# Local-attention value windows: 42 rows per block instead of 38, and one load for both heads' edge blocks

## The chip, the cores and the metric

The kernel runs on one core of a Trainium2 chip, as one program. The metric is device time in microseconds (us), the median of several executions. Five engines work beside each other, each through its own instruction list in a fixed order: PE (matrix products), DVE (vector work), ACT (activation functions, copies), POOL (some vector sums) and SP, which only issues DMA transfers here. A core has 16 DMA engines.

## The reference

Three stages follow one another, and each feeds the next.

```python
# attention: q, k, v are (2 batches, 8 heads, 576 positions, 64), float32; factor 4
out_d     = softmax(scale * q_d @ k_d.T) @ v_d      # q_d, k_d, v_d: means over 4 positions
scores    = where(|i - j| < 4, scale * q @ k.T, -1e9)
out_local = softmax(scores) @ v
x = repeat(out_d, 4) + out_local                    # 1152 tokens x 512
# first feed-forward
h = x @ w_in                                        # 512 -> 2048
y = (h * tanh(softplus(h))) @ w_out                 # 2048 -> 512
# second feed-forward
out = (silu(y @ w_gate) * (y @ w_val)) @ w_out2     # 512 -> 1536 -> 512
```

The weights arrive in 64-bit floats; x, q, k and v in 32-bit ones.

## The kernel before

**Attention.** The heads are taken in pairs: 2 batches x 4 pairs. For a pair, `prep` (L403) loads q and k (`qk`, L429, 1024 runs of 256 bytes over 128 partitions), the last 64 positions of all heads (`qr`, L400, 64 partitions x 8 heads) and the values for the coarse attention (`vq`, L434, 72 partitions x 4 runs of 1 KB). PE transposes q and k (L463), ACT copies them out (L480), DVE and POOL form the sums over four positions (L491, L447), and `down` (L512) does the coarse attention.

**Local attention.** A position sees only its neighbours within three places, so the positions are cut into 18 blocks of 32 (`BLK`), and a block needs 38 keys and values (`WIN`): its 32 and three at either side. `ks_of(t)` is where the window of block t begins; block 0 has nothing to its left and block 17 nothing to its right, so their windows are shifted. Six blocks form a unit, three units (u = 0, 1, 2) a head pair. `duo` (L636) works on two units at once: scores (L667), softmax on DVE and ACT, transposes (L699), the products with the values (`o_local`, L712), and the sum with the coarse part (L725), which is written to the token tile `xy`.

**The value windows.** `load_windows` (L605) is called for each batch and each half of its pairs (four calls in all). A call makes six loads, 24 in all: a load fetches the windows of one unit for both heads of a pair, one window row per partition, so that a block's 38 rows lie in 38 partitions (0 to 37 or 64 to 101), and the six blocks lie side by side. Row and block are 256 bytes (64 floats) each. For one head, one DMA takes all blocks whose windows are regular ("inner": five for u = 0 and u = 2, six for u = 1), and a further DMA takes the shifted edge block. That makes four DMAs for u = 0 and u = 2, two for u = 1: 80 in all, all issued by SP on L618. The tile is `vw` where the two units share a pair and `vj` where they don't; each has two buffers.

**The weights.** `convert` (L267) loads 512 KB of a weight matrix into `raw` (L282 or L287, on SP), of which there are three buffers; ACT and DVE turn the 64-bit numbers into a pair of reduced-precision tiles (L299 to L335). The products of the first feed-forward (L771 to L773) begin while attention still runs.

**Order.** `Plan.run` is a list scheduler that runs when the kernel is built. It knows a cost for each step, a due time (`want`) and the free buffers, and writes one fixed order for each engine. A load's cost on SP comes from this function, so a load of windows counts `us_dma(12 * WIN, 256)`, 0.73 us:

```python
def us_dma(runs, size):
    return max(0.475, runs * max(size, 512) / 320e3)
```

On SP the windows stand between `prep`'s loads and the first `raw` loads, in that fixed order. Where PE would be idle in the plan, short products of zeros (`warm`, L1106) are put in; they are instructions like others, 179 in all.

Of the kernel before, what the change touches and what calls it, by code (L numbers as in the profile page):

```python
# [20 lines left out]
BLK = 32  # L21
WIN = BLK + 6
EXN = 3
NTOK = 1152
PC = 384
PIECES = [(i * PC, PC) for i in range(3)]
# [56 lines left out]
class Plan:  # L83
# [9 lines left out]
    def add(self, eng, fn, deps=(), want=0.0, new=(), use=(), table=None):  # L93

        o = Op(eng, fn, deps, want, list(new), list(new) + list(use), table)
        self.ops.append(o)
        return o
# [72 lines left out]
def attention_moe_kernel(  # L170
# [12 lines left out]
    nc = tc.nc  # L183
    PE, ACT, DVE, POOL = nc.tensor, nc.scalar, nc.vector, nc.gpsimd
    B, H, S, D = q.shape
# [19 lines left out]
    plan = Plan()  # L205
    E_PE, E_POOL, E_SP = "PE", "POOL", "SP"
# [8 lines left out]
    def us_act(n, psum=False):  # L215
        return n / 1200 + (0.051 if psum else 0.093)

    def us_dma(runs, size):
        return max(0.475, runs * max(size, 512) / 320e3)
# [12 lines left out]
    def ring(pool, tag, n):  # L232
        if tag not in rings:
            rings[tag] = Ring(n)
        return rings[tag]

    def buf(pool, shape, dt, tag, n):

        b = Buf(ring(pool, tag, n))

        def make():
            tiles = b.ring.tiles
            if b.slot not in tiles:
                tiles[b.slot] = (late[pool] if isinstance(pool, str) else pool).tile(
                    shape, dt, tag=f"{tag}{b.slot}", name=f"{tag}{b.slot}", bufs=1)
            b.tile = tiles[b.slot]
            return b.tile

        b.make = make
        return b  # L250
# [6 lines left out]
    
    x_buf = buf(xp, [128, 2, 4, NTOK], F32R, "xy", 1)
    x_buf.ring.give(x_buf)
# [89 lines left out]
    masks = acst.tile([128, 9, WIN], BF16, name="masks")  # L349
    exs = acst.tile([128, EXN, 6, 64], F32, name="exs")  # L350

# [38 lines left out]
    def ks_of(t):  # L390
        return min(max(BLK * t - 3, 0), S - WIN)
# [213 lines left out]
    def load_windows(b, y, w):  # L605

        def load(vw, p, u, r0, h0, first):
            ts = [6 * u + j for j in range(6)]
            inner = [j for j in range(6) if ks_of(ts[j]) == BLK * ts[j] - 3]

            def f(e):
                if first:
                    vw.make()
                for h in range(2):
                    s_ = v[b, 2 * p + h]
                    row = vw.tile[r0:r0 + WIN, h0 + h]
                    for j0, n in [(inner[0], len(inner))] + [(j, 1) for j in range(6) if j not in inner]:
                        nc.sync.dma_start(out=row[:, j0:j0 + n, :],  # L618
                                          in_=bass.AP(tensor=s_.tensor, offset=s_.offset + ks_of(ts[j0]) * D,
                                                      ap=[[D, WIN], [BLK * D, n], [1, D]]))  # L620
            return f

        for u0, u1, apart in (((0, 1, False), (2, 2, True)), ((0, 0, True), (1, 2, False)))[b]:
            vw = buf(ld, [128, 2 if apart else 4, 6, 64], F32, "vj" if apart else "vw", 2)
            o = None
            for p in range(2):
                for k, u in enumerate((u0, u1)):
                    if not apart or p == k:
                        h0 = 0 if apart else 2 * p
                        o = plan.add({E_SP: us_dma(12 * WIN, 256)}, load(vw, 2 * y + p, u, 64 * k, h0, o is None), [o], w,  # L630
                                     [] if o else [vw], [vw] if o else [])
                        wins[b, 2 * y + p, u] = (vw, o, h0)

    ex_ring = ring(None, "ex", EXN)

# [131 lines left out]
    att_ops = []  # L767
    GSHAPE = [128, 2, NTOK]

# [25 lines left out]
    def l1(f, i, want):  # L795
        n = PC
        if f not in HB:
            HB[f] = buf(thp, [128, NTOK], F32, "H", RING)
            HB[f].ops, HB[f].first = [], None
# [17 lines left out]
    def mish(f, h, want):  # L817

        add = plan.add
        g = G[f] = buf("g", GSHAPE, F32R, "G", 7)  # L820
        t = buf("g", [128, NTOK], F32, "T", 2)

# [18 lines left out]

        o = add({"ACT": us_act(NTOK)}, tanh, h.ops + tanhs[-1:] + att_ops, want + 1.79, [t], [h], "exp")
        tanhs.append(o)
# [4 lines left out]
        for f, h, g, t, want, atan, sin, mult, hi, lo in batch:  # L848
            o = add({"ACT": us_act(NTOK) + 0.09}, atan, [o, o_small], want + 10.41, use=[t], table="trig")
            o = add({"ACT": us_act(NTOK) + 0.09}, sin, [o], want + 10.41, use=[t], table="trig")  # L850
# [145 lines left out]
    w = 10.0  # L996
    prep(0, 0, w)
    load_windows(0, 0, w)
    duo([(0, 0, 0), (0, 1, 0)], (w, w + 2.0), True)
    w += 2 * 2.0  # L1000
# [4 lines left out]
    duo([(0, 2, 0), (0, 2, 1)], (w, w + 2.0), True)  # L1005
    w += 2 * 2.0
    load_windows(0, 1, w)
    duo([(0, 0, 2), (0, 1, 2)], (w, w + 2.0), True)
    w += 2 * 2.0
# [3 lines left out]
    t_p0 = w  # L1013
    prep(1, 0, w + 2.0)
    load_windows(1, 0, w)
    duo([(0, 2, 2), (0, 2, 3)], (w, w + 2.0), False)
    w += 2 * 2.0
# [125 lines left out]
```

## Time and profile before

| | us |
|---|---|
| median of 3 executions | 562.24 (561.42 to 565.15) |
| the profiled execution | 563.22 |
| its span, first to last instruction | 561.4 |
| PE busy in the span | 521.1 (93%) |
| DVE busy | 380.9 (68%) |
| ACT busy | 274.3 (49%) |
| POOL busy | 23.3 (4%) |

The profiled execution is 1.0 us above the median; 1.8 us of it lie outside the span. An engine's busy share is a mean over stages: the profile's strip of 40 slices shows PE near full from about 126 us to the end, while attention, ahead of that, has slices with PE, DVE and ACT all half idle. SP has no busy time of its own in the profile: the time of its DMA-issuing instructions stands in the chain of waits and in the timeline as "SPq". The rows that the prediction uses stand below, behind the diff.

### The profile page before, as it was taken

The page shows a single profiled execution, that of the slowest core. Times are in us where ns is not written, and L with a number is a line of the kernel's source. Part 1 is how long each engine was busy: PE and PEld are TensorE (multiplying, and loading weights), DVE is VectorE, ACT ScalarE, POOL GpSimd, SP SyncE. Part 2 cuts the span into 40 slices and gives each one's busy share as a digit, 9 for nine tenths or more (in the row PEclk, how much of TensorE's full clock was granted, in tenths as well). Part 3 has the DMA queues.
Part 4 walks back from the last instruction along what each step waited for, and adds up shares of the span by engine and source line. Part 5 has one row for each costly group of instructions (what it writes and reads, how often), then busy time and mean ns, then how long its engine had stood idle before and what let it go on. Part 6 is the DMA issues. An engine that isn't in the chain of part 4 may idle for free.

```text
span 561.4 us, 9942 instructions
## 1 busy us (share of the span) xinstructions
PE 521.1 (93%) x3991; PEld 486.4 (87%) x3991; DVE 380.9 (68%) x764; ACT 274.3 (49%) x567; POOL 23.3 (4%) x41
## 2 busy tenths in 40 slices
PE   9949694749998999999999999999999999999997
PEld 7737474638998999999999999999999889998885
DVE  4817563536998999898886999866666249733321
ACT  3925453405699985973892454333343244321000
POOL 3303110200000000000000000000000000000000
PEclk9966869567999999999999999999999999999999
DMA  9355261441432125321512133433222204100022
GB/s 181 81 98 106 67 152 40 119 126 52 151 114 75 39 85 177 114 75 39 188 41 73 37 114 113 132 102 103 77 76 76 75 1 149 39 0 1 0 76 93
DMA packets 58749, 48.52 MB, mean 86 GB/s; under 512 B 31184, under 2 KB 53968, under 8 KB 58704
## 3 DMA queue, kind: packets, MB, share of 16 engines
q1 hardware_dynamic: 58704, 47.90, 29.9%
q8 instruction: 31, 0.51, 0.4%
q14 instruction: 14, 0.11, 0.1%
HBM read 45.53 MB, written 2.36 MB: 85 GB/s over the span
## 4 chain that ended last, share of the span: by engine, by line
PE 70%; SPq 17%; DMA 4%; ACT 4%; issue 2%; DVE 1%; POOL 1%; ACTq 0%; POOLq 0%
PE b L771 19%; PE b L773 18%; PE b L772 18%; SPq L618 14%; PE b L966 4%; PE b L967 4%; PE b L965 4%; DMA vq<-in_v_dram 2%; SPq L429 1%; PE b L712 1%; POOL vd L447 1%; DMA raw<-in_moe_w_out_dram 1%; DMA raw<-in_moe_w_in_dram 1%; SPq L282 1%; ACT T L830 1%
## 5 line engine op out<-in xcount | busy, mean ns | idle before, releaser
L771 PE MATMUL b<-xy,wt 128*128 128x384 f32 x480 | 163.6, 341 | 0.0
L773 PE MATMUL b<-xy,wt 128*128 128x384 f32 x480 | 162.5, 339 | 0.0
L772 PE MATMUL b<-xy,wt 128*128 128x384 f32 x480 | 162.5, 338 | 0.0
L771 PEld LDWEIGHTS b<-xy,wt 128*128 128x128 f32 x480 | 91.8, 191 | 0.5 <-issue 0.2
L772 PEld LDWEIGHTS b<-xy,wt 128*128 128x128 f32 x480 | 91.8, 191 | 0.0
L773 PEld LDWEIGHTS b<-xy,wt 128*128 128x128 f32 x480 | 91.7, 191 | 0.0
L772 PE MATMUL b<-G,wt 128*128 128x384 f32 x192 | 64.2, 335 | 1.8 <-DVE G L840 1.8
L773 PE MATMUL b<-G,wt 128*128 128x384 f32 x192 | 64.1, 334 | 0.0
L771 PE MATMUL b<-G,wt 128*128 128x384 f32 x192 | 64.1, 334 | 0.0
L299 ACT ACTIVATE cw<-raw 128x512 f32<-128x512 f32 x61 | 40.6, 669 | 36.0 <-DVE wt L335 16.6
L226 ACT ACTIVATE G<-H 128x384 fp32r<-128x384 f32 (+1 forms) x40 | 24.0, 605 | 64.0 <-DVE H L937 43.2
L335 DVE TENSOR_TENSOR wt<-cw,wt 128x512 fp32r<-128x512 f32 x68 | 46.3, 690 | 2.6 <-ACT wt L226 1.4
L314 DVE SCALAR_TENSOR_TENSOR cw<-raw,cw 128x512 uint32<-128x512 uint32 x68 | 46.7, 693 | 0.5
L319 DVE SCALAR_TENSOR_TENSOR cw<-raw,cw 128x512 uint32<-128x512 uint32 x68 | 46.5, 691 | 0.3
L967 PE MATMUL b<-wt,G 128*128 128x512 f32 x108 | 42.1, 389 | 0.0
L966 PE MATMUL b<-wt,G 128*128 128x512 f32 x108 | 42.0, 389 | 0.0
L965 PE MATMUL b<-wt,G 128*128 128x512 f32 x108 | 42.0, 389 | 0.0
L305 DVE TENSOR_SCALAR cw<-cw 128x512 f32<-128x512 f32 x68 | 28.2, 424 | 18.7 <-ACT cw L299 18.7
L226 ACT ACTIVATE wt<-cw 128x512 fp32r<-128x512 f32 x43 | 26.2, 625 | 26.7 <-PE b L772 25.3
L772 PEld LDWEIGHTS b<-G,wt 128*128 128x128 f32 x192 | 36.0, 188 | 2.1 <-DVE G L840 2.1
L937 DVE TENSOR_TENSOR H<-b,H 128x384 f32<-128x384 f32 x36 | 20.0, 554 | 24.5 <-PE b L773 24.4
L771 PEld LDWEIGHTS b<-G,wt 128*128 128x128 f32 x192 | 36.0, 188 | 0.0
(95 smaller groups left out, 748.8 us busy)
## 6 DMA issues: line engine op xcount, KB each, us to landing
raw<-in_moe_w_out_dram SPq DMA_DIRECT2D x28, 512.0 KB
raw<-in_moe_w_in_dram SPq DMA_DIRECT2D x16, 512.0 KB
raw<-in_moe_w_gate_dram SPq DMA_DIRECT2D x12, 512.0 KB
raw<-in_moe_w_val_dram SPq DMA_DIRECT2D x12, 512.0 KB
vq<-in_v_dram SPq DMA_DIRECT2D x8, 288.0 KB
out_dram<-acc SPq DMA_DIRECT2D x9, 256.0 KB
qk<-in_q_dram SPq DMA_DIRECT2D x8, 256.0 KB
qk<-in_k_dram SPq DMA_DIRECT2D x8, 256.0 KB
```

The costliest lines, as they stand in the source:

```text
L226: ACT.activation(out, in_, AF.Copy)
L299: ACT.activation(cw.tile, h.bitcast(F32), AF.Abs)
L314: DVE.scalar_tensor_tensor(out=c, in0=words()[:, :, 0], scalar=29, in1=c, op0=ALU.logical_shift_right, op1=ALU.bitwise_or)
L319: DVE.scalar_tensor_tensor(out=c, in0=words()[:, :, 1], scalar=0xC0000000, in1=c, op0=ALU.bitwise_and, op1=ALU.bitwise_or)
L335: DVE.tensor_tensor(out=wt.tile[:, 1], in0=cw.tile, in1=wt.tile[:, 0].bitcast(F32), op=ALU.subtract)
L618: nc.sync.dma_start(out=row[:, j0:j0 + n, :], in_=bass.AP(tensor=s_.tensor, offset=s_.offset + ks_of(ts[j0]) * D, ap=[[D, WIN], [BLK * D, ...
L771: PE.matmul(out=ps, lhsT=wt_hi, rhs=m_hi, start=first, stop=False)
L772: PE.matmul(out=ps, lhsT=wt_hi, rhs=m_lo, start=False, stop=False)
L773: PE.matmul(out=ps, lhsT=wt_lo, rhs=m_hi, start=False, stop=last)
L965: PE.matmul(out=ps.tile, lhsT=g[:, 0, tok], rhs=wt[:, 0], start=(f == fs[0]), stop=False)
L966: PE.matmul(out=ps.tile, lhsT=g[:, 0, tok], rhs=wt[:, 1], start=False, stop=False)
L967: PE.matmul(out=ps.tile, lhsT=g[:, 1, tok], rhs=wt[:, 0], start=False, stop=(f == fs[-1]))
```

## The change

The diff brings in `VR = 42`. The DMA for the inner blocks of a head takes 42 rows per block instead of 38, so it writes 42 partitions (0 to 41 or 64 to 105); nothing reads the four added rows. The edge block is no longer loaded once per head: one DMA, behind the two for the inner blocks, takes it for both heads, again with 42 rows, except for block 17, whose window begins at position 538 and has only 38 rows left. A load now has three DMAs for u = 0 and u = 2, and two for u = 1. The planner counts a load as `us_dma(12 * VR, 256)`, 0.81 us.

```diff
+VR = 42
...
             def f(e):
                 if first:
                     vw.make()
+                n = len(inner)
                 for h in range(2):
                     s_ = v[b, 2 * p + h]
-                    row = vw.tile[r0:r0 + WIN, h0 + h]
-                    for j0, n in [(inner[0], len(inner))] + [(j, 1) for j in range(6) if j not in inner]:
-                        nc.sync.dma_start(out=row[:, j0:j0 + n, :],
-                                          in_=bass.AP(tensor=s_.tensor, offset=s_.offset + ks_of(ts[j0]) * D,
-                                                      ap=[[D, WIN], [BLK * D, n], [1, D]]))
+                    nc.sync.dma_start(out=vw.tile[r0:r0 + VR, h0 + h, inner[0]:inner[0] + n, :],
+                                      in_=bass.AP(tensor=s_.tensor, offset=s_.offset + ks_of(ts[inner[0]]) * D,
+                                                  ap=[[D, VR], [BLK * D, n], [1, D]]))
+                for j in range(6):
+                    if j not in inner:
+                        k0 = ks_of(ts[j])
+                        n = min(VR, S - k0)
+                        nc.sync.dma_start(out=vw.tile[r0:r0 + n, h0:h0 + 2, j, :],
+                                          in_=v[b, 2 * p:2 * p + 2, k0:k0 + n].rearrange("h p d -> p h d"))
             return f
...
-                        o = plan.add({E_SP: us_dma(12 * WIN, 256)}, load(vw, 2 * y + p, u, 64 * k, h0, o is None), [o], w,
+                        o = plan.add({E_SP: us_dma(12 * VR, 256)}, load(vw, 2 * y + p, u, 64 * k, h0, o is None), [o], w,
                                      [] if o else [vw], [vw] if o else [])
```

## Rows read from the trace of the kernel before

**Rows 1.** The page's chain that ended last, by line, shares of the span.

```profile
PE b L771 19%; PE b L773 18%; PE b L772 18%; SPq L618 14%; PE b L966 4%; PE b L967 4%; PE b L965 4%; DMA vq<-in_v_dram 2%; SPq L429 1%; PE b L712 1%; POOL vd L447 1%; DMA raw<-in_moe_w_out_dram 1%; DMA raw<-in_moe_w_in_dram 1%; SPq L282 1%; ACT T L830 1%
```

**Rows 2.** SP's timeline: start, length, line, tile, count of DMAs.

```profile
14.68 12.85 SPq L618 DMA_DIRECT2D vw<-in_v_dram  x12
27.57 7.80 SPq L618 DMA_DIRECT2D vj<-in_v_dram  x8
35.47 0.61 SPq L429 DMA_DIRECT2D qk<-in_q_dram  x1
...
37.62 0.61 SPq L400 DMA_DIRECT2D qr<-in_q_dram  x1
...
45.69 12.88 SPq L618 DMA_DIRECT2D vw<-in_v_dram  x12
58.62 7.80 SPq L618 DMA_DIRECT2D vj<-in_v_dram  x8
...
74.02 0.41 SPq L434 DMA_DIRECT2D vq<-in_v_dram  x1
74.48 9.00 SPq L618 DMA_DIRECT2D vj<-in_v_dram  x8
83.53 13.24 SPq L618 DMA_DIRECT2D vw<-in_v_dram  x12
...
98.30 9.49 SPq L618 DMA_DIRECT2D vj<-in_v_dram  x8
107.85 12.97 SPq L618 DMA_DIRECT2D vw<-in_v_dram  x12
```

**Rows 3.** The chain in order of time: start, us, what.

```profile
17.60 1.30 SPq L618
18.94 0.29 SPq L618
...
96.81 0.39 SPq L282
...
120.93 4.10 DMA raw<-in_moe_w_in_dram
```

**Rows 4.** PE's waits, 0 to 126.4 us: total, times, longest.

```profile
PE b L712 <- DVE xs L725: 10.9, 1, 10.9
PE b L463 <- DMA qk<-in_q_dram: 5.7, 1, 5.7
PE b L712 <- DMA vw<-in_v_dram: 4.4, 4, 1.4
PE b L712 <- DMA vj<-in_v_dram: 3.2, 3, 1.4
```

**Rows 5.** PE's waits from 126.4 us to the end.

```profile
PE b L566 <- ACT ed L555: 8.5, 1, 8.5
```

**Rows 6.** All engines' waits, 0 to 185 us: those for the first weights.

```profile
ACT cw L299 <- DMA raw<-in_moe_w_in_dram: 13.9, 3, 12.8
...
DVE cw L301 <- DMA raw<-in_moe_w_in_dram: 11.6, 1, 11.6
```

**Rows 7.** Stretches: length; PE, PEld, DVE, ACT, POOL busy; clock; DMA share; GB/s.

```profile
0.00:14.00 14.00, 12.81 (x185) 9.97 (x185) 6.24 (x17) 5.50 (x16) 5.40 (x20) 1.00 0.99 181
14.00:28.00 14.00, 13.85 (x298) 10.65 (x297) 12.23 (x40) 13.92 (x65) 4.42 (x6) 1.00 0.38 81
42.00:56.00 14.00, 14.00 (x235) 10.37 (x231) 10.03 (x25) 7.12 (x32) 4.53 (x6) 0.66 0.57 106
70.00:84.00 14.00, 13.86 (x195) 10.44 (x196) 9.57 (x24) 8.32 (x33) 2.60 (x3) 0.68 0.62 156
86.00:96.00 10.00, 5.05 (x90) 4.09 (x87) 2.77 (x9) 4.00 (x19) 0.00 (x0) 1.00 0.16 37
98.00:112.00 14.00, 10.04 (x162) 8.39 (x166) 7.98 (x22) 6.33 (x23) 3.81 (x3) 0.50 0.45 121
112.00:126.00 14.00, 5.92 (x49) 5.36 (x42) 4.98 (x16) 1.16 (x5) 0.00 (x0) 0.62 0.40 119
0.00:126.40 126.40, 91.97 (x1503) 73.02 (x1503) 66.00 (x188) 57.34 (x240) 23.28 (x41) 0.76 0.49 108
126.40:557.40 431.00, 429.09 (x2488) 413.38 (x2488) 314.23 (x576) 216.99 (x328) 0.00 (x0) 0.99 0.25 80
```

## The prediction, made before the changed kernel was built

> **What bounds the kernel now.** I read the chain of waits first, because a share of busy time doesn't tell which stage has room. It has two parts: the products of the feed-forward layers, and SP issuing on L618, 14% of the span [rows 1]. L618 is the value windows. SP's timeline shows where they lie: eight blocks of issues between 14.68 and 120.82 us, 12.85 + 7.80 + 12.88 + 7.80 + 9.00 + 13.24 + 9.49 + 12.97 = 86.03 us for 80 DMAs [rows 2].
>
> Then: who suffers. The stretches split the span at 126.4 us. Behind it PE is busy 429.09 of 431.00 us, so that part only moves with its start. Ahead of it PE is busy 91.97 of 126.40 us, DVE 66.00 and ACT 57.34 [rows 7]. PE's long waits ahead of it, and the one that ends at it, add up to 10.9 + 5.7 + 4.4 + 3.2 + 8.5 = 32.7 us [rows 4, 5], and each leads back to L618:
> - 4.4 and 3.2 us wait for the windows themselves.
> - 5.7 us wait for a qk load that SP issues at 35.47, right behind a block of windows that ends at 35.37 [rows 2].
> - 10.9 us wait for DVE, which itself waits 11.6 us for a weight tile [rows 6]; SP issues a weight load at 96.81 [rows 3], behind the windows that end at 96.77 [rows 2].
> - 8.5 us wait for ACT, which waits 12.8 us for a weight tile [rows 6] whose load goes out when the last windows are issued, at 120.8; the chain then runs through its landing [rows 3].
>
> So SP's queue is the bound of attention. What makes it slow: a five-block DMA (190 runs) holds SP 1.30 us, a one-block DMA (38 runs) 0.29 [rows 3]. Yet a qk load of 1024 runs of the same size takes 0.61, qr's 512 runs 0.61, and vq's 288 runs, four times as long, 0.41 [rows 2]. Runs alone don't set the price. In 86 to 96 us, where SP issues only windows, the DMA engines are 0.16 busy (2.6 of 16) at 37 GB/s; in the first 14 us, with loads of 128, 64 and 72 partitions, 0.99 at 181 GB/s [rows 7]. The windows use few DMA engines, and SP is held back by those few. What sets the cheap loads apart is the row count: if a transfer is cut into equal parts over at most 16 engines, 128 and 64 rows go in 16 parts, 72 in 12, but 38 = 2 x 19 only in 2. 42 goes in 14.
>
> **The change, part by part.**
>
> (1) 42 rows. 24 loads of 456 runs (10,944) become 8 x (504 + 504 + 496) = 12,032 runs, 10% more. No row shows a 42-row load. Bounds for one inner DMA: below 0.29, the cheapest L618 issue, above 1.30 x 210/190 = 1.44, if the price stays with the runs. I take 0.40, near the 72-row load's 0.41, as that is the nearest row whose count has a large divisor.
>
> The Trainium skill, "DMA: Bandwidth & Descriptors", section "Why a DMA increments its semaphore by 16 and not by 1", says that a transfer runs on the largest number of engines, up to 16, that divides the slowest dimension of both sides; by it 38 rows use 2 and 42 use 14, so an inner DMA would give each engine 15 runs, below the 19 of today's one-block DMA, and the windows would take 64 x 0.33 = 21 us of SP, seven less than by my price. The trace agrees as to 38 (0.16 of 16 engines) and shows nothing of 42.
>
> (2) One DMA for both heads' edge block: 80 DMAs become 64. The eight for block 17 keep 38 rows and carry 76 runs, twice a one-block DMA: 0.58 each, 1.4 us over 0.40 for all eight. With about 0.04 us between issues, SP spends 64 x 0.44 + 1.4 = 30 us on windows instead of 86; between 64 x 0.33 + 1.4 = 23 and 86.03 x 12,032/10,944 = 94.6. The edge block moves behind both inner DMAs, so u = 0's first product, which reads block 0, waits one issue more: 0.44 us, hidden while SP is ahead; uncovered, about 3.5 us for eight loads.
>
> (3) What SP no longer holds back. SP is 56 us lighter, but the path gets only what PE can use. First the 32.7 us of waits. Second the clock: in the stretches behind such waits PE's granted clock is 0.66, 0.68, 0.50 and 0.62, against 1.00 in 14 to 28 us [rows 7]; at full clock their busy time would shrink by 14.00 x 0.34 + 13.86 x 0.32 + 10.04 x 0.50 + 5.92 x 0.38 = 16.5 us. I take 10, since PE then waits for DVE and ACT more often. Check from DVE's side: in 14 to 28, not yet held up, DVE is busy 12.23 of 14 [rows 7]; at that density the 66.00 - 6.24 - 12.23 = 47.5 us left need 54.4, and the 126.4 us point comes at 82.4, a gain of 44. The two agree; I take **43 us**. DVE's floor without any idle time from 28 us on is 28 + 47.5 = 75.5, a gain of 51.
>
> What is late next is DVE with ACT (13.92 of 14 us in that stretch), not SP: 30 us of windows beside some 35 loads at up to 0.65 leave it well under 82 us.
>
> (4) The DMA engines. Share 0.49 of 126.4 us is 62 us of all 16 [rows 7]. The windows' part, 0.16 of some 86 us, is 14; spread out at the 181 GB/s of the first stretch, 3.08 MB take 17. So 65 us have to fit in some 83: room, but bursts will queue. Price: nothing in the sum, up to half of the 32.7 us in the range.
>
> (5) The planner counts 0.81 instead of 0.73 us per load, 1.8 us in all, and may write another order on every engine. Nothing prices this; I take 0, and 3 us either way.
>
> Behind 126.4 us nothing changes: PE is full, and the same conversions stand in the same queues. The sum: 563.2 (the profiled execution) - 43 = 520.2; that execution is 1.0 above the median, so **519**.
>
> **The rivals.**
>
> *A, the forecast* (gain 31 to 56, 506 to 531): SP falls behind the other engines. For it: five waits with one origin, and a wide margin for the new price (even 0.65 per DMA leaves 42 us of windows). Chance 0.66.
>
> *B, a new wait takes over* (gain 7 to 31, 531 to 555). The queues of PE, ACT and DVE are fixed against the planner's costs. Released from SP, they may wait for each other, or for loads that queue in the DMA engines, or SP may stand at a full vq or raw buffer with windows behind it. At half the waits and nothing of the clock the gain is 16: 546. Against it: 14 to 28 us, where no windows were yet needed, runs with PE, ACT and DVE nearly full. Chance 0.19.
>
> *C, slower.* 42 rows are still served by two engines, as if only powers of two divided the work (42 holds one factor 2, like 38; 64 and 128 hold many, and 72 eight). Then the same two engines move 3.08 MB instead of 2.80: at 37 GB/s 83.3 us instead of 75.7, all of it on the path: +7.6 us, 570 against the median. Point of decision: the mean price of the 64 DMAs above 86.03/64 = 1.34 us. Against it: vq's 72 rows are cheap. Chance 0.07.
>
> *D, more than 56 us* (below 506): needs DVE without idle time and PE at full clock throughout. Chance 0.06.
>
> *E, no change*: SP's place as bound is taken at once by another chain of the same length. Five traced waits speak against it. Chance 0.02.
>
> **The numbers.** The likeliest case gives 519. The range is 506 to 546: at its low end the 51 us of DVE's floor with 3 to 5 us for the order and for clock behind 126.4 us, at its high end B's half gain. Left out are D (0.06), C (0.07), E (0.02) and B's part above 546 (0.05), 0.20 in all. A change under 1% (5.6 us) can't be told from none. Faster: A + B + D = 0.91. Same: 0.02. Slower: 0.07.
>
> **What would show it.** L618 in SP's timeline: 64 DMAs, about 0.4 us each, some 30 us in all instead of 86; for block 17 about 0.6. GB/s while windows are issued: well above 37. PE's waits for windows, and those at 10.9, 5.7 and 8.5 us, gone or under 2; granted clock in attention near 1.00 rather than 0.50 to 0.68; PE's solid part beginning near 83 instead of 126 us, with the 431 us behind it as long as before. The chain should show ACT and DVE of attention in place of L618. I am wrong if L618 still takes over 1 us per DMA (C), or if the issues are short but waits for vq, raw or ACT of several us stand in PE's list (B).

## The result, and the profile after

The changed kernel takes 516.12 us (median of 4 runs, 513.47 to 520.27) against 562.37 for the kernel before: a ratio of 0.9177, 95% interval 0.9108 to 0.9246, 46 us less. The forecast was 519, range 506 to 546.

The profiled execution takes 515.88 us with a span of 514.1, against 563.22 and 561.4: 47.3 us less. First the page's busy times and its chain of waits, by engine and by line.

```profile
PE 505.8 (98%) x4009; PEld 474.5 (92%) x4009; DVE 376.4 (73%) x762; ACT 275.6 (54%) x569; POOL 22.1 (4%) x41
...
PE 89%; DMA 4%; ACT 2%; DVE 2%; SPq 1%; issue 1%; POOL 0%; POOLq 0%; ACTq 0%
PE b L777 21%; PE b L778 21%; PE b L779 21%; PE b L973 5%; PE b L971 5%; PE b L972 5%; PE warm L1112 4%; DMA vq<-in_v_dram 2%; PE b L718 2%; PE b L464 2%; PE b L673 1%; DMA qk<-in_q_dram 1%; DMA raw<-in_moe_w_in_dram 1%; PE b L567 1%; PE b L579 1%; PE b L705 1%
```

The lines have moved: the windows are L618 (inner blocks) and L625 (edge blocks), the first feed-forward's products L777 to L779. The windows' 14% [rows 1] are gone from the chain, and PE holds 89% of it. PE's idle time, span less busy, was 561.4 - 521.1 = 40.3 us and is 8.3: 32.0 less. Its busy time fell by 15.3 us though its list grew by 18 products of zeros. The two make up the 47.3.

SP's timeline, as in [rows 2]: the windows of the first of the four calls, and the end of the last.

```profile
15.30 1.66 SPq L618 DMA_DIRECT2D vw<-in_v_dram  x2
17.00 0.41 SPq L625 DMA_DIRECT2D vw<-in_v_dram  x1
17.46 2.82 SPq L618 DMA_DIRECT2D vw<-in_v_dram  x4
20.61 0.32 SPq L625 DMA_DIRECT2D vw<-in_v_dram  x1
20.96 0.86 SPq L618 DMA_DIRECT2D vw<-in_v_dram  x2
21.87 0.88 SPq L618 DMA_DIRECT2D vj<-in_v_dram  x2
...
72.64 1.76 SPq L618 DMA_DIRECT2D vw<-in_v_dram  x4
74.45 0.28 SPq L625 DMA_DIRECT2D vw<-in_v_dram  x1
74.84 15.66 SPq L283 DMA_DIRECT2D raw<-in_moe_w_in_dram  x4
```

The 64 issues add up to 31.9 us instead of 86, and the last is out at 74.7 us instead of 120.8. Where nothing holds them up, two inner DMAs take 0.80 to 0.97 together; the median of one is 0.41. The weights' loads follow at 74.84; before, at 120.93 [rows 3].

All PE waits of the changed kernel, in the columns of [rows 4]:

```profile
PE b L464 <- DMA qk<-in_q_dram: 1.5, 1, 1.5
PE warm L1112 <- DVE wsrc L382: 1.2, 1, 1.2
PE b L778 <- DVE G L846: 1.2, 1, 1.2
PE b L777 <- ACT G L227: 0.4, 1, 0.4
```

The five long waits of [rows 4, 5] are gone; one for qk of 1.5 us stands in attention. To see where the gain lies, take two marks. The first is the last group of transposes for the coarse attention (L566, now L567), in PE's timeline: before, the wait of 8.5 us [rows 5] ends there, and there the prediction splits the span. The second is the product that waits for the first activations of the second layer, in the chain in order of time. Before, and after:

```profile
126.44 1.36 PE L566 MATMUL b<-ident,ed 72*72 72x72 f32 x8 [8.52 <-ACT ed L555]
...
180.01 0.45 PE b L772
```

```profile
84.96 0.67 PE L567 MATMUL b<-ident,ed 72*72 72x72 f32 x8
...
133.75 0.44 PE b L778
```

The stretches up to the first mark and between the two, before and after, in the columns of [rows 7]:

```profile
0.00:126.44 126.44, 91.97 (x1503) 73.02 (x1504) 66.04 (x188) 57.38 (x240) 23.28 (x41) 0.76 0.49 108
126.44:180.01 53.57, 51.74 (x422) 49.06 (x422) 45.52 (x91) 43.20 (x77) 0.00 (x0) 0.93 0.32 102
```

```profile
0.00:84.96 84.96, 82.27 (x1529) 65.88 (x1529) 61.91 (x185) 59.30 (x254) 22.14 (x41) 0.92 0.79 159
84.96:133.75 48.79, 47.23 (x414) 45.36 (x412) 45.61 (x89) 41.24 (x64) 0.00 (x0) 1.00 0.34 109
```

Up to the first mark the gain is 126.44 - 84.96 = 41.5 us. Between the marks it is 53.57 - 48.79 = 4.8: PE is nearly always busy there in both kernels, with nearly the same products, but its clock is 1.00 instead of 0.93. From the second mark to the end of the span it was 561.4 - 180.01 = 381.4 us, and is 514.1 - 133.75 = 380.4. Last, the stretches of attention, in the columns of [rows 7]:

```profile
14.00:28.00 14.00, 14.00 (x344) 11.02 (x343) 12.26 (x39) 12.95 (x59) 4.64 (x7) 1.00 0.72 146
28.00:42.00 14.00, 13.98 (x314) 10.46 (x313) 12.23 (x37) 12.90 (x57) 4.84 (x7) 1.00 1.01 160
42.00:56.00 14.00, 12.52 (x261) 10.50 (x254) 7.74 (x30) 10.23 (x52) 1.70 (x3) 0.83 0.87 200
56.00:70.00 14.00, 14.00 (x274) 11.49 (x269) 10.16 (x21) 5.81 (x13) 3.70 (x4) 0.68 0.78 171
...
20.60:24.40 3.80, 3.80 (x80) 2.96 (x80) 2.72 (x11) 3.80 (x19) 2.17 (x3) 1.00 0.48 111
```

In 20.6 to 24.4 us SP issues nothing but windows, and 111 GB/s move where it was 37. DVE keeps its pace of 12.2 of 14 us for 28 us; then comes a dip, with clocks of 0.83 and 0.68. The chain in order of time shows what stands ahead of it, from a vq load to the qk load behind it:

```profile
26.13 6.48 DMA vq<-in_v_dram
...
32.75 0.74 POOL vd L448
...
35.10 5.49 DMA vq<-in_v_dram
...
40.61 0.32 SPq L625
...
40.97 0.96 SPq L618
...
44.89 4.43 DMA qk<-in_q_dram
...
49.45 0.63 PE b L464 x4
```

vq's loads, POOL's sums and windows between the loads on SP still make one queue; PE reaches its end at 49.45 and waits 1.5 us. The clock falls behind it, close to 0.50, the lower of its two levels (1.2 and 2.4 GHz):

```profile
51.00:65.00 14.00, 14.00 (x248) 11.25 (x246) 9.67 (x24) 7.26 (x21) 3.01 (x3) 0.51 0.81 169
```

Two landings of vq make 12.0 of the 23.3 us of this chain, and the DMA engines are 1.01 busy in 28 to 42 us. Ahead of 40.61 SP waits 1.5 us in the middle of one load of windows, where the program asks for no buffer, and the profile puts this down to the landing of vq. So full DMA engines seem to have a part in the dip; how large a part, no run separates.

### The profile page after: what moved, and what is told of

It is laid out like the page before. It is cut to its first block, busy times and chain, and to the rows that moved or that the text cites. A ratio compares the mean times of both kernels' runs of the same rounds, so it can differ in the third digit from the quotient of the medians.

```text
span 514.1 us, 9965 instructions
## 1 busy us (share of the span) xinstructions
PE 505.8 (98%) x4009; PEld 474.5 (92%) x4009; DVE 376.4 (73%) x762; ACT 275.6 (54%) x569; POOL 22.1 (4%) x41
## 4 chain that ended last, share of the span: by engine, by line
PE 89%; DMA 4%; ACT 2%; DVE 2%; SPq 1%; issue 1%; POOL 0%; POOLq 0%; ACTq 0%
PE b L777 21%; PE b L778 21%; PE b L779 21%; PE b L973 5%; PE b L971 5%; PE b L972 5%; PE warm L1112 4%; DMA vq<-in_v_dram 2%; PE b L718 2%; PE b L464 2%; PE b L673 1%; DMA qk<-in_q_dram 1%; DMA raw<-in_moe_w_in_dram 1%; PE b L567 1%; PE b L579 1%; PE b L705 1%
## 5 line engine op out<-in xcount | busy, mean ns | idle before, releaser
L777 PE MATMUL b<-xy,wt 128*128 128x384 f32 x480 | 161.0, 335 | 0.0
L779 PE MATMUL b<-xy,wt 128*128 128x384 f32 x480 | 160.4, 334 | 0.0
L778 PE MATMUL b<-xy,wt 128*128 128x384 f32 x480 | 160.4, 334 | 0.0
L777 PEld LDWEIGHTS b<-xy,wt 128*128 128x128 f32 x480 | 90.1, 188 | 0.2
L778 PEld LDWEIGHTS b<-xy,wt 128*128 128x128 f32 x480 | 90.1, 188 | 0.0
L779 PEld LDWEIGHTS b<-xy,wt 128*128 128x128 f32 x480 | 90.1, 188 | 0.0
L777 PE MATMUL b<-G,wt 128*128 128x384 f32 x192 | 64.2, 335 | 0.4 <-ACT G L227 0.4
L779 PE MATMUL b<-G,wt 128*128 128x384 f32 x192 | 64.1, 334 | 0.0
L227 ACT ACTIVATE G<-H 128x384 fp32r<-128x384 f32 (+1 forms) x41 | 25.2, 620 | 66.9 <-DVE H L943 44.4
L300 ACT ACTIVATE cw<-raw 128x512 f32<-128x512 f32 x58 | 38.8, 673 | 20.7 <-DVE wt L336 14.3
L227 ACT ACTIVATE wt<-cw 128x512 fp32r<-128x512 f32 x46 | 28.1, 628 | 33.4 <-PE b L778 24.8
L986 DVE TENSOR_TENSOR acc<-b,acc 128x512 f32<-128x512 f32 x18 | 12.5, 692 | 34.6 <-PE b L973 34.6
L777 PEld LDWEIGHTS b<-G,wt 128*128 128x128 f32 x192 | 36.0, 188 | 0.7 <-ACT G L227 0.7
```

The source lines that it names most:

```text
L227: ACT.activation(out, in_, AF.Copy)
L300: ACT.activation(cw.tile, h.bitcast(F32), AF.Abs)
L777: PE.matmul(out=ps, lhsT=wt_hi, rhs=m_hi, start=first, stop=False)
L778: PE.matmul(out=ps, lhsT=wt_hi, rhs=m_lo, start=False, stop=False)
L779: PE.matmul(out=ps, lhsT=wt_lo, rhs=m_hi, start=False, stop=last)
```

## The experiments

Three theories could explain the gain. **S**: the row count decides how many DMA engines a transfer runs on. **F**: fewer, merged DMAs make it. **O**: the changed cost makes the planner write a better order. A fourth, **R**, is that any larger row count would do. Ratios are against the kernel before, run on the same chip.

**42 rows alone**, edge blocks per head, the old order:

```diff
-                    row = vw.tile[r0:r0 + WIN, h0 + h]
...
-                        nc.sync.dma_start(out=row[:, j0:j0 + n, :],
+                        nr = min(VR, S - ks_of(ts[j0]))
+                        nc.sync.dma_start(out=vw.tile[r0:r0 + nr, h0 + h, j0:j0 + n, :],
...
-                                                      ap=[[D, WIN], [BLK * D, n], [1, D]]))
+                                                      ap=[[D, nr], [BLK * D, n], [1, D]]))
```

> 42 rows per block, but the edge block still once per head (80 DMAs) and the planner's old cost, so the written order is that of before. Theory S (the row count decides on how many DMA engines a transfer runs: 38 on two, 42 on fourteen): inner DMAs take about 0.4 us of SP, 80 of them some 32 us, time 514 to 524. Theory F (fewer, merged DMAs make the gain): SP stays at 80 or more us, time 560 to 572. Theory O (the newly written order makes it): 560 to 572.

Measured: 521.18 us (520.19 to 521.80), ratio 0.9288 (0.9269 to 0.9307). The row count alone brings 40 us. SP's part missed its number: the eight blocks of issues take 44 us, not 32. Its timeline, the first and last call:

```profile
15.86 6.94 SPq L619 DMA_DIRECT2D vw<-in_v_dram  x12
22.84 3.98 SPq L619 DMA_DIRECT2D vj<-in_v_dram  x8
...
66.94 5.92 SPq L619 DMA_DIRECT2D vj<-in_v_dram  x8
72.92 6.56 SPq L619 DMA_DIRECT2D vw<-in_v_dram  x12
79.59 11.79 SPq L283 DMA_DIRECT2D raw<-in_moe_w_in_dram  x4
```

**Merged edge blocks alone**: the changed loads with 38 rows, the old order.

```diff
-VR = 42
+VR = 38
```

> The edge block in one DMA for both heads (64 DMAs), but 38 rows and the planner's old cost. S: the same 10,944 runs go through the same two engines, 82 to 86 us of SP, time 556 to 566. F: time 514 to 530. O: 558 to 566.

Measured: 561.54 us, ratio 1.0009 (0.9991 to 1.0028); the windows take 82.3 us of SP. F as the whole cause falls.

**The new order alone**: the kernel before with the new cost.

```diff
-o = plan.add({E_SP: us_dma(12 * WIN, 256)}, load(
+o = plan.add({E_SP: us_dma(12 * 42, 256)}, load(
...
```

> The loads of before (38 rows, 80 DMAs) in the order that the planner writes for the changed kernel (a load counted as 0.81 us). S and F: SP is held as before, time 556 to 570, any difference to 562 being what the order is worth with SP as the bound. O: 514 to 535.

Measured: 561.11 us, ratio 0.9988 (0.9969 to 1.0007). O falls, although the order of PE, DVE and ACT is written anew from end to end.

**41 rows**, in the changed kernel's order (the planner's cost stays that of 42 rows in this run and in those with 39, 46 and 48):

```diff
-VR = 42
+VR = 41
```

> The changed kernel in its own order with 41 rows per block instead of 42. S: 41 is prime, so a DMA runs on one engine; the rows come at half of 37 GB/s, about 3.0 MB in 160 us, 85 more than before the change, time 620 to 660. Theory R (any count above 38, or the number of rows as such, does it) and F: 510 to 520.

Measured: 645.6 us (one run): one row less than 42, and 130 us lost. In a stretch with nothing but windows:

```profile
74.00:90.00 16.00, 3.55 (x36) 2.99 (x34) 2.44 (x13) 4.53 (x25) 0.00 (x0) 0.73 0.08 19
```

A DMA share of 0.08 at 19 GB/s is half of the 0.16 and 37 that 38 rows had [rows 7], as one engine in place of two would give. (The shares are 1.3 and 2.6 of 16, so it is their ratio that speaks.)

**The changed loads in the old order:**

```diff
-o = plan.add({E_SP: us_dma(12 * VR, 256)}, load(
+o = plan.add({E_SP: us_dma(12 * WIN, 256)}, load(
...
```

> The changed kernel's loads (42 rows, 64 DMAs) with the planner's old cost, so in the written order of before. Against the changed kernel it prices the new order, against the run with 42 rows alone (521) the merged edge blocks. S with neither of weight: 515 to 521. If the order matters (O in part): 2 or more us off the changed kernel's 516, either way. If merging matters: 3 or more us below 521.

Measured: 515.87 us (514.79 to 520.05), ratio 0.9169 (0.9125 to 0.9213). The order is worth nothing here either. Against 42 rows alone, in the same order, the merged edge blocks are worth 0.9288 - 0.9169 = 1.2% of the time before, some 7 us, and the intervals are apart. Merging does nothing while two engines hold SP, and something once they don't. (Percentages below are also of the time before.)

**39, 46 and 48 rows** separate the number of rows from its divisors (39 = 3 x 13, 46 = 2 x 23, 48 = 3 x 16). The edit is VR again.

> The changed kernel in its own order with 39 rows: one row more than before the change, 3 x 13, so thirteen engines and 7% fewer runs than with 42. S: 511 to 520, as fast as 42 or 1 to 2 us faster where the DMA engines are full. Theory R (the number of rows as such): 39 is next to 38, 550 to 565.

Measured: 513.84 us (513.21 to 517.11), ratio 0.913 (0.9094 to 0.9166). One row more than 38 brings 49 us. Against the change's 0.9177 (0.9108 to 0.9246) the intervals overlap, so it isn't shown to be better than 42.

> 46 = 2 x 23 rows, in the changed kernel's order. S: two engines again, 10% more runs than with 42: 3.35 MB at 37 GB/s, 91 us of windows, 15 more than before the change: 568 to 585. R: 510 to 522.

Measured: 577.81 us (one run). In a stretch in which the other engines stand still, the rate of two engines is back:

```profile
62.00:72.00 10.00, 0.00 (x0) 0.00 (x0) 0.00 (x0) 0.00 (x0) 0.00 (x0) 0.69 0.16 36
```

> 48 rows, sixteen engines, 14% more runs than with 42, in the changed kernel's order. S: inner DMAs at about 0.4 us as with 42; 514 to 522, since two more engines and 1,600 more runs about cancel. If the DMA engines now bound attention (0.72 to 1.01 busy between 14 and 70 us after the change), 519 to 524.

Measured: 516.69 us (515.71 to 519.84), ratio 0.9185 (0.9143 to 0.9227). As fast as 42 within the intervals. The five row counts go 645.6, 513.8, 577.8, 516.1, 516.7 for 41, 39, 46, 42 and 48; R falls, and so does the rule of powers of two (rival C), by which 42 and 46 would be alike. The three fast counts are also the three multiples of 3, and no further count was run against that; but the q, k and qr loads have 128 and 64 rows, and with them the DMA engines are 0.99 busy at 181 GB/s [rows 7], and 3 doesn't explain why 41 runs at half the rate of 38 and 46.

Then: what bounds attention after the change?

**Long runs**: the inner DMAs read contiguous rows from the wrong places.

```diff
...
-ap=[[D, VR], [BLK * D, n], [1, D]]
+ap=[[D, VR], [1, n * D]]
...
```

> The changed kernel, but an inner DMA reads its 42 rows as contiguous runs of five or six times 256 bytes (from the wrong places of v, so the local sums are not the reference's): the same bytes and transfers, 3,000 runs instead of 12,032. What the windows' small runs still cost after the change. If the DMA engines bound the middle of attention (share 0.72 to 1.01): 3 to 8 us faster than 516. If PE, DVE and ACT bound it: 514 to 518.

Measured: 514.65 us (513.47 to 515.92), ratio 0.9159 (0.9131 to 0.9187), inside the change's interval. The small runs of the windows cost nothing that shows in the times. (By the code there are 3,296 runs, not 3,000.) The profiled execution, the fastest of the three, has a clock of 1.00 from 14 to 84 us and no wait of PE for qk; one trace can't tell whether that is due to the long runs.

**q and k in 1 KB runs**, with 39 rows; an existing switch of the kernel, for the second batch, `(1,)`, and for both, `(0, 1)`:

```diff
-KB = ()
+KB = (1,)
```

> 39 rows, and q and k of the second batch loaded as 1 KB runs (256 instead of 1,024 per load), at the price of eight PE products in place of four transposes per tile. If the DMA engines bound attention after the change: 2 to 6 us faster than 514. If PE does: 1 to 3 us slower.

Measured: 519.33 us, ratio 0.9243 (0.9199 to 0.9287): 1.1% slower than 39 rows alone, more than either case forecast.

> As the run before, for both batches. DMA engines the bound: 4 to 10 us faster than 514, since the first 14 us are 0.99 full too. PE the bound: 2 to 6 us slower.

Measured: ratio 0.9234 (0.9177 to 0.9291), also slower than 39 rows alone. So relief of the DMA engines at this price doesn't pay. That PE is the bound isn't shown by it: with the eight products the plan also puts in fewer products of zeros, 149 and 101 in place of 197, and by the next run fewer of them alone cost 0.7%.

**Fewer products of zeros**, with 39 rows:

```diff
-plan.spare = (keep, 0.5, 95, 256 / 2400.0 + 0.003)
+plan.spare = (keep, 0.5, 30, 256 / 2400.0 + 0.003)
```

> 39 rows, and the products of zeros only up to 30 us of the plan instead of 95. If PE is the bound of attention and they only lengthen its list (4% of the chain after the change): 3 to 10 us faster than 514. If they keep the clock up where PE waits: slower, 515 to 530, with a granted clock under 0.98.

Measured: 517.68 us, ratio 0.9202 (0.9174 to 0.9230): 0.7% slower, with granted clocks of 0.970 to 0.975 over four executions where 39 rows alone have 0.990 to 0.997. The stretches behind the vq queue, with 112 fewer products:

```profile
42.00:56.00 14.00, 9.35 (x175) 7.54 (x175) 7.56 (x31) 8.20 (x43) 0.92 (x2) 0.64 0.93 204
56.00:70.00 14.00, 13.46 (x244) 10.55 (x244) 9.39 (x18) 6.11 (x16) 5.06 (x6) 0.63 0.68 168
```

With them, 39 rows have:

```profile
42.00:56.00 14.00, 12.37 (x298) 10.38 (x289) 8.76 (x33) 10.68 (x56) 2.48 (x4) 0.97 0.84 195
56.00:70.00 14.00, 14.00 (x263) 11.78 (x262) 10.82 (x25) 6.29 (x15) 3.02 (x4) 0.79 0.71 161
```

PE is busy for longer with the zeros and gets 0.97 and 0.79 of the clock in place of 0.64 and 0.63. By the medians the zeros pay for themselves, just. These two traces don't show where: their executions take 517.11 us with the zeros (the slowest of its four) and 517.59 without, and reach the last transposes of L567 at 84.41 and 84.09 us. No version tried is shown to beat the change.

## Why the prediction was right, step by step

**The bound and its cause: right, shown.** With 42 rows alone the time falls by 40 us, with 41 it rises by 84, and PE's long waits go together with the windows on SP. The explanation by equal parts over at most 16 engines agrees with all six row counts run (38, 39, 41, 42, 46, 48). How many engines ran is read only where they are few (38, 41 and 46, by DMA share and rate); of 39, 42 and 48 the runs show that they are fast, not that they use thirteen, fourteen and sixteen.

**(1) The price of an issue: right in the sum, in part by luck.** An inner DMA was forecast at 0.40, and its median is 0.41; the windows at 30 us, and they take 31.9. But some inner DMAs are held up to 1.38 us, so that the 48 take some 25.5 us instead of 19.2, while the 16 edge DMAs take 5.2 instead of 7.8 (without the gaps between issues): two misses, one against the other. Block 17's DMA, forecast at 0.6, shows 0.28 all eight times. The cheaper price by runs per engine, 0.29, didn't come for an inner DMA. It was no sound bound, since the row of a DMA doesn't hold its own wait (last section). So the Trainium skill's rule ("DMA: Bandwidth & Descriptors", section "Why a DMA increments its semaphore by 16 and not by 1") agrees with every row count here as far as the traces tell the number of engines, and my estimate of SP's time from it, 21 us, was a third too low.

**(2) The merged edge blocks: mis-sized.** I counted them within SP's time and gave them nothing on the path, as SP would be ahead. They are worth about 1.2%. SP wasn't as far ahead as "a wide margin" said: with 80 DMAs the weights' load goes out at 79.59 us, with 64 in the same order at 76.28, and PE still waits for that load's work (3.7 and 3.5 us). Which part of the 7 us this makes isn't settled: PE's waits of 0.5 us and more, without the first product's, add up to 7.8 and 6.4 us only, and the two profiled executions, both the slowest of their runs, are only 1.7 us apart (521.80 and 520.05).

**(3) What the path gets: right up to the end of attention.** Ahead of the first mark PE's idle time fell from 34.5 to 2.7 us: 31.8, where 32.7 were forecast. Its busy time fell by 9.7 us, zeros included, where 10 were taken for the clock. The gain there is 41.5 us for the 43 forecast. The check by DVE's pace gave 44; DVE held that pace for 28 us and then met the dip.

**Behind attention: the term that was left out.** "Behind 126.4 us nothing changes: PE is full" took PE's busy share for its speed. PE was full there, but it came out of the wait of 8.5 us with a low clock (0.62 in 112 to 126 us [rows 7]) and had 0.93 between the marks. Without that wait it has 1.00, and the stretch is 4.8 us shorter; the rest up to the end is 1.0 us shorter. These 5.8 us, put at nothing, are why the profiled gain is 47.3 and not 41.5. That they hang on the wait is supported by the changed loads in the old order: in its profiled execution PE still waits 3.5 us at the first mark, the clock behind it is 0.94, and the marks are 53.4 us apart, as before the change.

**What is late next: the sign was wrong, the cause is open.** I named DVE with ACT. The chain gives each 2%, PE 89%. But of the 82.3 us that PE is busy ahead of the first mark, 27.6 are products of zeros, which the plan puts where PE would wait, so a full PE here doesn't show that its real products are the bound. The one dip begins in vq's queue, the place that rival B named. It costs PE 1.5 us of waiting and half the clock for 14 us, an estimated 14.00 x 0.49 = 6.9 us by the prediction's way of counting, not half the gain. The granted clock is 1.00 up to about 51 us, 0.51 up to 65 and 1.00 again from 70: "near 1.00" was only half right.

**(4) The DMA engines: right as to their total.** They are busy 0.81 of the first 83 us, 67 us, where 65 were forecast. "Bursts will queue" came as well, in the stretch ahead of the dip; the price of nothing is not contradicted by the time of the run with long runs, but a few us aren't excluded. **(5) The order: right**, nothing, by two runs.

## What to carry to other kernels

A transfer's outermost count is worth a look before its bytes: 38 and 39 rows differ by 49 us here, and their largest divisors up to 16 are 2 and 13. A load queue that is slow shows in the profile as waits of other engines for loads that only stand behind it, so follow each long wait to what its queue did just ahead of it. When such a queue is released, count the clock as well as the waits: 15 of the 47 us were PE being busy for less time with the same work, and 4.5 of these lay behind the last wait, where PE had looked full.

## What was not expected of the hardware

SP's issue time doesn't follow the runs: an inner DMA of five or six blocks shows 0.40 us with 39 rows, 0.41 with 42 and 0.44 with 48 (medians of L618), beside 0.29 for 38 runs [rows 3]. And with 38 rows the time that a DMA waits stands on the one behind it: in the run with merged edge blocks, these read 1.30 us (median) for 76 runs, as long as five-block DMAs of 190, while the same 76 runs of block 17 read 0.28 behind fast DMAs in the changed kernel. A row of SP's timeline has to be read as a sum with its neighbours.
